# A linear-attention and expert-routing kernel: own terms moved to the scores' diagonal, router logits from turned outputs, state product on quarters of the array

## The chip, the cores and the metric

The kernel runs on one core of a Trainium2 chip. The time is the device time of one execution in microseconds (us); three runs of the kernel before gave a median of 439.97 us (439.43 to 441.21). The engines named below are PE (TensorE, the matrix engine; PEld is its loading of weights), DVE (VectorE), ACT (ScalarE), POOL (GpSimd) and SP (SyncE, which here only issues transfers). All data is fp32.

## The reference, cut to what matters

```python
# attention part: B=4, H=8 heads, S=768 tokens, D=48
for t in range(S):
    kt, vt, rt = k[:, :, t], v[:, :, t], r[:, :, t]
    cur = np.einsum('bhd,bhe->bhde', u[None] * kt, vt)          # the token's own term
    y[:, :, t] = np.einsum('bhd,bhde->bhe', rt, state + cur)
    state = w[None, :, :, None] * state + np.einsum('bhd,bhe->bhde', kt, vt)
x = y.transpose(0, 2, 1, 3).reshape(3072, 384)                  # a token's row: 8 heads of 48

# expert part: 4 groups of 4 experts, each 384 -> 1024 -> 384
g_idx = argmax(x @ w_group)                 # 384 x 4
e_idx = argmax(x @ w_expert[g_idx])         # 384 x 4 for each group
gate  = softmax of the group, at g_idx, times softmax of the expert, at e_idx
out   = gate * (relu(x @ w1[g_idx, e_idx]) @ w2[g_idx, e_idx])
```

The attention is computed in chunks of 128 tokens. Within a chunk, token t takes from an earlier token j of the chunk a score (r_t against k_j with decays) times v_j; from earlier chunks it takes r_t against the state; from itself it takes (sum over d of r*u*k) times v_t. That last part is the own term.

## The kernel before

There are 24 tiles (6 chunks of 4 batches), each of 128 tokens and 8 heads. The program runs in steps; in step s it works on several tiles at once, each at another stage: `turn(s)`, `scores(s-1)`, `values(s-2)`, `back(s-3)`, `rows_T(s-4)` and `row_logits(s-5)`. Two heads of 64 padded rows share the 128 rows of a tile; HP = 4 is the number of such pairs, DP = 64 the padded width of a head, P = 128, KO = 3.

```python
def own(g):                                    # for a pair of tiles; on POOL
    nc.gpsimd.tensor_mul(dg, rts[...], kts[...])
    nc.gpsimd.tensor_mul(dg, dg, spread(ub, 1, 2))
def own_sum(g):
    nc.vector.reduce_sum(out=du, in_=dg, axis=AX)
def own_values(n):                             # the own term, one per head: 8 on ACT
    for h in range(H):
        nc.scalar.mul(dv[:, h, :], v[:, a, h, 0:D], du[:, a, h : h + 1])

def turn(n):                                   # 8 transposes
    transposes of r into pr, of k into pk
    nc.vector.tensor_mul(rT, pr, T1T[m])
    nc.scalar.copy(kT, pk)

def scores(n):
    for hc in range(HP):
        for e in range(2):
            nc.tensor.matmul(pa[e][:, hc, :], lhsT=kT[rows of e, hc, :], rhs=rT[rows of e, hc, :])
    for e in range(2):
        nc.vector.tensor_mul(am[:, e], pa[e], spread(later, 1, HP))   # keeps earlier tokens only

def values(n):
    if c > 0:                                  # the state's part: four products on the whole array
        for hc in range(HP):
            nc.tensor.matmul(py[:, hc, :], lhsT=R[b][:, hc, :], rhs=rT[:, hc, :], ...)
    for hc in range(HP):
        for e in range(2):
            nc.tensor.matmul(py[64 * e : 64 * (e + 1), hc, :], lhsT=v of head 2hc+e, rhs=am[:, e, hc, :])
    nc.scalar.copy(yT, py)
    ...                                        # not in the last chunk: the state's update
    8 products into pu (64 rows x 48 columns)
    for e in range(2):
        nc.vector.tensor_add(state of e, pu[rows of e], state of e)   # or add and multiply

def back(n):
    4 transposes of yT into pb
    nc.vector.tensor_add(xts[c][:, b, 0:DM], pb, dv)                  # here the own term comes in
def rows_T(n):
    3 transposes of the row tile into px
    nc.scalar.copy(xT, px)
def row_logits(n):                             # 384 x 20 weights of the router, in three parts
    for ko in range(KO):
        nc.tensor.matmul(pl, lhsT=xT[:, ko, :], rhs=gw[:, ko, :], ...)
```

Every four tiles (in the last chunk every two) the router runs: `choice` (some 12 DVE instructions), `exps` (ACT), `before` (two PE products that count tokens), `gate` and `place` (8 DVE instructions), and `rows` (one indirect transfer on POOL for each tile, which writes token rows into the regions of their experts). After the last tile come, with `up(0, ...)` and `down(0, ...)`, the first 128 rows of the fullest expert, which were already written, and then sixteen items of up to 256 rows, one for each expert. PSUM tiles of the tag `bank` share six buffers in turn.

Of the kernel before, what the change touches and what calls it, by code (L numbers as in the profile page):

```python
# [15 lines left out]
P = 128  # L16
# [18 lines left out]
def kernel(  # L35
# [105 lines left out]
    def load_pair(g, k_queue=nc.sync):  # L141

        load(r, g, rts[g % RING][:, :, :, 0:D])
        load(k, g, kts[g % RING], k_queue)
        load(v, g, vts[g % (RING + 1)][:, :, :, 0:D])
# [21 lines left out]

    idle = bank([P, P], "idle")
# [19 lines left out]
    R = ring([P, HP, P], "R", B)  # L188
# [92 lines left out]
    gw = cst([P, KO, NL], "gw")  # L281

    def load_small():
        nc.sync.dma_start(out=gw[:, :, 0:G], in_=moe_w_group.rearrange("(ko p) g -> p ko g", p=P))
        for g in range(G):
            nc.sync.dma_start(
                out=gw[:, :, G + Eg * g : G + Eg * (g + 1)], in_=moe_w_expert[g].rearrange("(ko p) e -> p ko e", p=P)
            )
# [60 lines left out]
    def route(pool, rb, xt, T, sums, number, group, apart=False):  # L349
# [28 lines left out]
        def choice():  # L378
            nc.vector.reduce_max(out=mx, in_=L, axis=AX)

# [4 lines left out]
            nc.vector.reduce_max(out=kx, in_=key, axis=AX)  # L385
            nc.vector.tensor_tensor(out=ohg, in0=key[:, :, 0, :], in1=spread(kx[:, :, 0], 2, Eg), op=OP.is_equal)
# [5 lines left out]
            nc.vector.tensor_sub(ex, L, spread(mx, 3, Eg))  # L392
# [41 lines left out]
        return choice, exps, before, gate, place, rows  # L434
# [10 lines left out]
    w2_parts = wpool.tile([P, FO, KO, P], FP32, name="w2_parts")  # L445

# [22 lines left out]
    def logits(xT, pl):  # L469
        for ko in range(KO):  # L470
            nc.tensor.matmul(pl, lhsT=xT[:, ko, :], rhs=gw[:, ko, :], start=(ko == 0), stop=(ko == KO - 1))
# [78 lines left out]
    def up(i, f, beside=None):  # L550
# [15 lines left out]

        behind = {2: (0,), 4: (2,), 6: (4, 6)} if i > 1 else {4: (0, 2), 6: (4, 6)}
        if i != 1:
            w2 = weights[ITEMS[i][0]][1]
            for a in behind.get(f, ()):  # L570
                nc.scalar.copy(w2_parts[:, a : a + 2], w2[:, a : a + 2, :].rearrange("p f (c k) -> p f k c", k=KO))  # L571
# [74 lines left out]
    dgs, dvs = {}, {}  # L646
    rkT, ams, yTs, xts, lgs, xTs = {}, {}, {}, {}, {}, {}
# [5 lines left out]
    def own(g):  # L653

        dg = dgs[g] = pool.tile([P, 2, H, D], FP32, tag="dg", name="dg")
        nc.gpsimd.tensor_mul(dg, rts[g % RING][:, :, :, 0:D], kts[g % RING])  # L656
        nc.gpsimd.tensor_mul(dg, dg, spread(ub, 1, 2))

    def own_sum(g):
        du = dvs[g] = pool.tile([P, 2, H], FP32, tag="du", bufs=2, name="du")  # L660
        nc.vector.reduce_sum(out=du, in_=dgs.pop(g), axis=AX)  # L661

    def own_values(n):
        g, a = n // 2, n % 2
        dv = dvs[g, a] = pool.tile([P, H, D], FP32, tag="dv", bufs=4, name="dv")
        for h in range(H):
            nc.scalar.mul(dv[:, h, :], vts[g % (RING + 1)][:, a, h, 0:D], dvs[g][:, a, h : h + 1])  # L667
# [17 lines left out]
    def scores(n):  # L685
        kT, rT = rkT[n]
        am = ams[n] = pool.tile([P, 2, HP, P], FP32, tag="am", bufs=2, name="am")
# [8 lines left out]
        for e in range(2):  # L696
            nc.vector.tensor_mul(am[:, e], pa[e], spread(later, 1, HP))  # L697

    def values(n):
# [5 lines left out]
        py = bank([P, HP, P], "py")  # L705
        if c > 0:
            for hc in range(HP):
                nc.tensor.matmul(
                    py[:, hc, :], lhsT=R[b][:, hc, :], rhs=rT[:, hc, :], start=(hc == 0), stop=False,
                    skip_group_check=True,  # L710
                )
        for hc in range(HP):
            for e in range(2):
                nc.tensor.matmul(  # L714
                    py[DP * e : DP * (e + 1), hc, :], lhsT=vt[:, a, 2 * hc + e, :], rhs=am[:, e, hc, :],
                    start=(c == 0), stop=True, skip_group_check=True,
                )
        yT = yTs[n] = pool.tile([P, HP, P], FP32, tag="yT", bufs=2, name="yT")
        nc.scalar.copy(yT, py)
# [9 lines left out]
        for e in range(2):  # L729
            rows = slice(DP * e, DP * (e + 1))  # L730
            state = R[b][rows, :, DP * e : DP * e + D]
            if c == 0:
                nc.vector.tensor_copy(state, pu[rows])
            elif c % SPAN < SPAN - 1:
                nc.vector.tensor_add(state, pu[rows], state)
            else:
                nc.vector.tensor_add(pu[rows], pu[rows], state)
                nc.vector.tensor_mul(state, pu[rows], spread(w_span[rows, :], 2, D))

    def back(n):  # L740

        c, b = tiles[n]
        yT = yTs.pop(n)
        if b == 0:
            xts[c] = pool.tile([P, B, XW], FP32, tag="xt", bufs=3, name="xt")
        pb = bank([P, HP, 2, DP], "pb")
        for hc in range(HP):
            nc.tensor.transpose(pb[:, hc].rearrange("p e d -> p (e d)"), yT[:, hc, :], ident)  # L748
        nc.vector.tensor_add(
            xts[c][:, b, 0:DM].rearrange("p (h d) -> p h d", h=H), pb.rearrange("p a e d -> p (a e) d")[:, :, 0:D],  # L750
            dvs.pop((n // 2, n % 2)),
        )

    def rows_T(n):
        xTs[n] = pool.tile([P, KO, P], FP32, tag="xT", bufs=2, name="xT")
        c, b = tiles[n]
        transposed(xts[c][:, b, 0:DM].rearrange("p (k d) -> p k d", d=P), xTs[n])
# [6 lines left out]
    def row_logits(n):  # L764
        last, i = GROUP[n]
        if i == 0:
            lgs[last] = route_bank()
        logits(xTs.pop(n), lgs[last][:, NL * i : NL * (i + 1)])
# [14 lines left out]
    own(0)  # L783
# [9 lines left out]
    LAST = 4  # L793
    for s in range(NT + LAST):
# [7 lines left out]
        if s % 2 == 0 and s // 2 + 2 < NP:  # L802
            load_pair(s // 2 + 2)
        if s == 1:
            load_small()
        if s in (3, 5, 7, 9):
            zero_places(s // 2 - 1)
        if s == FOUR * B + 6:
            pieces.append(("last", pick_first))
        if s == FOUR * B + 7:  # L810
# [3 lines left out]
        if s == FOUR * B + 10:  # L814
            columns(0)
        run("first")
        if s < NT:
            turn(s)
            if s % 2 == 1 and s // 2 + 1 < NP:
                if s > 1:  # L820
                    scale_k(s // 2 + 1, nc.gpsimd)
                own(s // 2 + 1)
        for n in range(NT):
            if s == n + 2 and n < NT - 1:
                own_values(n)
        run("choice")
        if 0 <= s - 4 < NT:
            rows_T(s - 4)
        n = s - 5
        if 0 <= n < NT:  # L830
            row_logits(n)
        if s == NT + LAST - 1:
            up(0, 2)
            row_logits(NT - 1)
        if 0 <= s - 3 < NT:
            back(s - 3)
# [3 lines left out]
        if s == FOUR * B + 7:  # L840
            load_rows(0, first, nc.sync)
            load_w2(first, 0)
            weights[0] = places[0]
        if 0 <= s - 1 < NT:
            scores(s - 1)
        if s == NT:
            own_values(NT - 1)
        if s == 1:
            own_sum(0)
        if s % 2 == 0 and 0 < s // 2 < NP:  # L850
            own_sum(s // 2)

# [9 lines left out]
        for n in (n, NT - 1) if s == NT + LAST - 1 else (n,):  # L862
            if n not in ROUTED:
                continue
            choice, exps, before, gate, place, rows = routing(n)
            T = ROUTED[n]
# [307 lines left out]
```

## Time and profile before

| what | value |
|---|---|
| time, median of 3 | 439.97 us |
| span of the profiled execution | 438.3 us |
| PE busy | 420.7 us (96%) |
| DVE busy | 187.6 us (43%) |
| ACT busy | 208.1 us (47%) |
| POOL busy | 198.8 us (45%) |
| first transposes of the last tile, first product of the first full item | 136.69 us, 172.31 us |

The page gives the busy time of each engine, the span cut into 40 slices with the busy share of each in tenths, and groups of instructions with their number, mean time and what they waited for. The timeline lists instructions by time: start, time to the end of the group, engine, line, operation, output and inputs, number. The ends of matrix products are modelled, and products overlap; so what counts in the timeline of PE is the distance between starts, not the length. A product of fp32 shows as two MATMUL records, a transpose as one. The attention takes roughly the first 150 us of the span, the experts the rest.

### The profile page before, as it was taken

What the parts mean: (1) busy time and instruction counts of PE and PEld (TensorE: products, weight loads), DVE (VectorE), ACT (ScalarE), POOL (GpSimd) and SP (SyncE); (2) the same over time, 40 slices, a digit from 0 to 9 for tenths busy, and PEclk for the clock granted to TensorE, in tenths of its full rate; (3) what the DMA queues carried; (4) which work ended last, traced back from release to release, by engine and by line L of the source; (5) the groups of instructions that cost most, each with busy time, mean ns of one, the idle gap of its engine ahead of it and who ended that gap; (6) DMA issues with size and microseconds to landing.
All of it is one profiled execution on the core that took longest, in us unless ns stands there. A gap on an engine that the chain in (4) does not pass through costs nothing. (4 is left out here: it accounts for less than half of the span.)

```text
span 438.3 us, 9515 instructions
## 1 busy us (share of the span) xinstructions
PE 420.7 (96%) x3463; PEld 406.4 (93%) x3463; DVE 187.6 (43%) x616; ACT 208.1 (47%) x482; POOL 198.8 (45%) x209
## 2 busy tenths in 40 slices
PE   6899999999999879999999999999999999999994
PEld 6788999999999879979999999999999999999993
DVE  6576578878777665312230330331331330332011
ACT  1885565555556524251542624615625633552560
POOL 7856546757474052421533614425425524532451
PEclk9999999999999999999999999999999999999998
DMA  9999999981014665999999998899998899999300
GB/s 169 233 251 218 275 270 204 216 162 38 20 38 118 163 247 118 270 212 234 269 221 233 260 257 203 228 239 215 240 254 207 237 266 214 250 264 220 123 24 27
DMA packets 126417, 86.63 MB, mean 198 GB/s; under 512 B 98982, under 2 KB 115509, under 8 KB 126364
## 3 DMA queue, kind: packets, MB, share of 16 engines
q1 hardware_dynamic: 114732, 69.08, 70.2%
q0 software_dynamic: 4960, 9.48, 7.1%
q10 hardware_dynamic: 6672, 7.41, 5.2%
q8 instruction: 28, 0.46, 0.5%
q14 instruction: 25, 0.20, 0.2%
HBM read 70.15 MB, written 16.44 MB: 198 GB/s over the span
## 5 line engine op out<-in xcount | busy, mean ns | idle before, releaser
L624 POOL DMA_INDIRECT out_dram<-yp,ids x104 | 101.1, 972 | 158.3 <-DVE yo L579 122.8
L585 PE MATMUL po<-hT,w_parts 128*128 128x128 f32 (+15 forms) x816 | 138.0, 328 | 1.6 <-ACT hT L565 1.0
L585 PEld LDWEIGHTS po<-hT,w_parts 128*128 128x128 f32 x816 | 133.5, 191 | 3.6 <-ACT hT L565 1.8
L617 DVE STREAM_TRANSPOSE yr<-yo 128x224 f32<-128x224 f32 (+3 forms) x48 | 21.9, 461 | 168.2 <-ACT yo L588 168.2
L561 PE MATMUL ph<-xe,w 128*128 128x128 f32 (+7 forms) x432 | 71.7, 326 | 0.8 <-PE pb L748 0.8
L561 PEld LDWEIGHTS ph<-xe,w 128*128 128x128 f32 x432 | 69.5, 194 | 1.3 <-PE pb L748 1.0
L588 ACT COPY yo<-po 128x128 f32<-128x128 f32 (+15 forms) x51 | 16.3, 320 | 112.2 <-PE po L585 112.2
L561 PE MATMUL ph<-xe,kall 128*128 128x240 f32 (+7 forms) x384 | 67.1, 335 | 0.0
L561 PEld LDWEIGHTS ph<-xe,kall 128*128 128x128 f32 x384 | 65.2, 190 | 0.6
L565 ACT ACTIVATE hT<-ph 128x256 f32<-128x256 f32 (+15 forms) x68 | 33.1, 494 | 39.1 <-PE ph L561 38.9
L667 ACT ACTIVATE dv<-vt,du 128x48 f32<-128x48 f32 x192 | 45.9, 324 | 1.8 <-DVE du L661 1.8
L571 ACT COPY w_parts<-rall 128x768 f32<-128x768 f32 x32 | 38.1, 1239 | 4.0 <-DMA rall<-in_moe_w_dram 4.0
L571 ACT COPY w_parts<-w 128x768 f32<-128x768 f32 x32 | 37.9, 1236 | 0.4 <-DMA w<-in_moe_w_dram 0.4
L427 POOL DMA_INDIRECT x_sorted<-xt,place_i x24 | 23.7, 988 | 24.8 <-DVE xe L526 12.9
L697 DVE TENSOR_TENSOR am<-pa,later 128x512 f32<-128x512 f32 x48 | 30.9, 685 | 8.9 <-PE pa L692 8.6
L656 POOL TENSOR_TENSOR dg<-rall,kall 128x768 f32<-128x768 f32 x12 | 21.8, 1821 | 25.2 <-DVE du L661 25.2
L651 POOL TENSOR_TENSOR kh<-kall,T 128x768 f32<-128x768 f32 (+1 forms) x12 | 21.5, 1798 | 18.7 <-DMA kall<-in_k_dram 14.2
L682 ACT COPY kT<-pk 128x512 f32<-128x512 f32 x24 | 14.0, 584 | 33.6 <-PE pk L678 27.8
L692 PE MATMUL pa<-rT,kT 48*128 48x128 f32 x384 | 28.4, 285 | 0.4 <-DVE rT L680 0.4
L714 PE MATMUL py<-am,vt 128*64 128x128 f32 x384 | 26.5, 279 | 0.0
L692 PEld LDWEIGHTS pa<-rT,kT 48*128 48x128 f32 x384 | 23.6, 187 | 2.2 <-DVE rT L680 0.6
L714 PEld LDWEIGHTS py<-am,vt 128*64 128x64 f32 x384 | 20.7, 136 | 3.2 <-issue 0.7
(139 smaller groups left out, 449.7 us busy)
## 6 DMA issues: line engine op xcount, KB each, us to landing
w<-in_moe_w_dram SPq DMA_DIRECT2D x32, 384.0 KB, 7.8
w<-in_moe_w_dram SPq DMA_DIRECT2D x8, 1536.0 KB, 7.0
kall<-in_moe_w_dram SPq DMA_DIRECT2D x32, 384.0 KB, 8.1
rall<-in_moe_w_dram SPq DMA_DIRECT2D x8, 1536.0 KB, 12.4
x_sorted<-nothing ACTq DMA_DIRECT2D x4, 1544.0 KB, 7.3
rall<-in_r_dram SPq DMA_DIRECT2D x12, 384.0 KB, 8.2
vt<-in_v_dram SPq DMA_DIRECT2D x12, 384.0 KB, 6.5
kall<-in_k_dram SPq DMA_DIRECT2D x10, 384.0 KB, 6.7
```

Of the source, the lines that this page charges most:

```text
L427: ins = nc.gpsimd.indirect_dma_start(out=xs_dram, out_offset=bass.IndirectOffsetOnAxis(ap=place_i[:, i : i + 1], axis=0), in_=xt[:, i, :], ...
L561: nc.tensor.matmul(ph[:, q, :], lhsT=w1[:, ko, P * (f + q) : P * (f + q + 1)], rhs=xe[:, ko, 0:w], start=(ko == 0), stop=(ko == KO - 1), s ...
L565: nc.scalar.activation(hTs[i][:, f : f + 2, 0:w], ph, AF.Relu)
L571: nc.scalar.copy(w2_parts[:, a : a + 2], w2[:, a : a + 2, :].rearrange("p f (c k) -> p f k c", k=KO))
L585: nc.tensor.matmul(po, lhsT=w2_parts[:, fo, d, :], rhs=hT[:, fo, 0:w], start=(fo == 0), stop=(fo == FO - 1))
L617: nc.vector.transpose(yr[:, 0:b, :, d], y[:, d, 0:w].rearrange("p (b t) -> p b t", t=BL))
L624: ins = nc.gpsimd.indirect_dma_start(out=out_pieces, out_offset=bass.IndirectOffsetOnAxis(ap=ids[:, j : j + 1], axis=0), in_=yp[:, j], in_ ...
L656: nc.gpsimd.tensor_mul(dg, rts[g % RING][:, :, :, 0:D], kts[g % RING])
L667: nc.scalar.mul(dv[:, h, :], vts[g % (RING + 1)][:, a, h, 0:D], dvs[g][:, a, h : h + 1])
L692: nc.tensor.matmul(pa[e][:, hc, :], lhsT=kT[rows, hc, :], rhs=rT[rows, hc, :], start=True, stop=True, skip_group_check=True,)
L697: nc.vector.tensor_mul(am[:, e], pa[e], spread(later, 1, HP))
L714: nc.tensor.matmul(py[DP * e : DP * (e + 1), hc, :], lhsT=vt[:, a, 2 * hc + e, :], rhs=am[:, e, hc, :], start=(c == 0), stop=True, skip_gr ...
```

## The change

Four things are done together.

- The own term goes onto the diagonal of the scores: ACT writes `ident * du` (8 instructions of 128 columns) into the score tile beforehand, and the DVE then copies the scores over it only where the token is earlier (`copy_predicated` in place of the multiplication with the mask). The output of `values` is then complete, and nothing has to be added in `back`.
- As yT is complete, the router's logits are taken from it: four products with weights of 32 columns, each on its own group of 32 columns of the array, one copy, one transpose and one DVE sum. The three transposes of the rows, their copy and three products go away, and with them one step of the pipeline (LAST = 3).
- The state is kept as 64 x 64 blocks, and its product runs as eight products on the four quarters of the array; yT is copied in two halves, the state's update is one instruction for 128 rows and not two for 64.
- `choice` is split into `choice` and `expert`, in two steps; the exponentials come after them. The end of the program is ordered anew; the router's weights are loaded earlier and in ten transfers of 48 partitions.

```diff
-def own_values(n):
-        for h in range(H):
-            nc.scalar.mul(dv[:, h, :], vts[...][:, a, h, 0:D], dvs[g][:, a, h : h + 1])
+def own_scores(n):
+        am = ams[n] = pool.tile([P, 2, HP, P], FP32, tag="am", bufs=2, name="am")
+        for e in range(2):
+            for hc in range(HP):
+                h = 2 * hc + e
+                nc.scalar.mul(am[:, e, hc, :], ident, dus[n // 2][:, n % 2, h : h + 1])
 # scores
-            nc.vector.tensor_mul(am[:, e], pa[e], spread(later, 1, HP))
+            nc.vector.copy_predicated(am[:, e], earlier, pa[e])
 # values
-            for hc in range(HP):
-                nc.tensor.matmul(py[:, hc, :], lhsT=R[b][:, hc, :], rhs=rT[:, hc, :], ...)
+            for j in range(2):
+                for o in range(2):
+                    for e in range(2):
+                        rows = slice(DP * e, DP * (e + 1))
+                        nc.tensor.matmul(py[e][DP * o : DP * (o + 1), j, :],
+                            lhsT=R[b][rows, 2 * o + j, :], rhs=rT[rows, 2 * o + j, :], ...)
 ...
-        nc.scalar.copy(yT, py)
+        for e in range(2):
+            nc.scalar.copy(yT[:, :, e, :], py[e])
 ...
-        for e in range(2):
-            ... nc.vector.tensor_add(state, pu[rows], state)
+        state = R[b][:, :, 0:D]
+        ... nc.vector.tensor_add(state, pu, state)
 # back
+        pl = bank([P, P], "pl")
+        for j in range(HP):
+            nc.tensor.matmul(pl[BL * j : BL * (j + 1), :], lhsT=gw[:, j, :], rhs=yT[:, j, :], start=True, stop=True)
+        nc.scalar.copy(lgT, pl)
 ...
-        nc.vector.tensor_add(xts[c][:, b, 0:DM], pb, dvs.pop(...))
+        nc.vector.tensor_copy(xts[c][:, b, 0:DM], pb)
-def rows_T(n): ...
 # row_logits
-        logits(xTs.pop(n), lgs[last][:, NL * i : NL * (i + 1)])
+        by_block = lgs[last][:, 512 - P : 512]
+        nc.tensor.transpose(by_block, lgTs.pop(n), ident)
+        nc.vector.reduce_sum(out=lgs[last][:, NL * i : NL * (i + 1)], in_=by_block by columns, axis=AX)
 # the loop over steps
-    LAST = 4
+    LAST = 3
+            if s == 0:
+                own(0, nc.vector, 0, 1)
+                own_sum(0, 0, 1)
+                own(0, nc.gpsimd, 1, 2)
-            load_pair(s // 2 + 2)
+            load_pair(s // 2 + 2, between=load_small if s == 0 else None)
 ...
+        if s == NT + 1:
+            for a in (0, 2):
+                w2_part(0, a, nc.gpsimd.tensor_copy)
```

Left out here: the places of the router's parts in the steps, the rest of the order at the end, and the changes of a branch that runs only when the decays are out of range.

## The prediction

> **What bounds the kernel now.** I read the slices of the span first, then the busy times of the attention stage, then one step of PE in the timeline, then the end of the attention.
>
> ```profile
> PE   6899999999999879999999999999999999999994
> DVE  6576578878777665312230330331331330332011
> ACT  1885565555556524251542624615625633552560
> ...
> 20.00:120.00 100.00, 98.93 (x1293) 93.09 (x1293) 74.71 (x185) 59.39 (x202) 58.66 (x38) 1.00 0.86 189
> ```
>
> A slice is 11 us. PE is full from slice 3 on, with a dent in slices 14 and 15 (153 to 175 us), where the attention hands over to the experts. From 20 to 120 us PE is busy 98.9 of 100 us, DVE 74.7, ACT 59.4, POOL 58.7. So the attention is bound by PE, with DVE next. From 172 us on nothing is changed. Now one step of PE:
>
> ```profile
> 70.40 0.66 PE L678 MATMUL pr<-ident,rall 128*128 128x128 f32 x4
> 70.89 0.60 PE L678 MATMUL pk<-ident,kh 128*128 128x128 f32 x4
> 71.33 0.49 PE L466 MATMUL px<-ident,xt 128*128 128x128 f32 x3
> 71.66 0.74 PE L471 MATMUL rb<-gw,xT 128*128 128x20 f32 x6
> 72.25 0.63 PE L748 MATMUL pb<-ident,yT 128*128 128x128 f32 x4
> 72.72 1.06 PE L708 MATMUL py<-rT,R 128*128 128x128 f32 x8
> 73.70 1.09 PE L714 MATMUL py<-am,vt 128*64 128x128 f32 x16
> 74.63 0.62 PE L725 MATMUL pu<-vt,kh 128*64 128x48 f32 x16
> 75.18 1.16 PE L692 MATMUL pa<-rT,kT 48*128 48x128 f32 x16
> 76.27 0.44 PE L678 MATMUL pr<-ident,rall 128*128 128x128 f32 x2
> ```
>
> A step takes 76.27 - 70.40 = 5.87 us. The distances between starts give the rate: 0.44 us for four transposes is 0.11 a pass; the products with R need about 0.11 a pass; the router's rb, only 20 columns wide, also need 0.59 / 6 = 0.10. py and pa run two passes at a time (16 in about 8 x 0.11), pu, 48 wide, in about 8 x 0.058. The rest is change of shape. Here are the last passes of pu and the first of pa:
>
> ```profile
> 75.02 0.23 PE L725 MATMUL pu<-vt,kh 128*64 128x48 f32 x2
> 75.18 0.38 PE L692 MATMUL pa<-rT,kT 48*128 48x128 f32 x2
> ```
>
> The first pa passes are 0.38 us long where a later one has 0.27, so in effect they begin at 75.29, 0.27 after the last pu. The same reading gives 0.26 from R to py and 0.27 from pa to pr. Passes of one shape follow at 0.11, so each change of the array's shape costs about 0.15 us.
>
> The sum for a step, in passes of 0.11: turn 8 (0.88), px and rb with their transitions 0.95, pb 4 (0.44), R 8 (0.90), py 8 pairs (0.88), pu 0.47, pa 8 pairs (0.90), and three changes of shape (0.45): 5.87. It closes.
>
> **What the Trainium skill says.** "TensorEngine Tiling (Array Packing)", section Key Properties: "Changing tiling mode (not just tile) drains the TensorE", while different tiles of one mode run in parallel. The trace agrees: 0.26 us against 0.11. "TensorE: Matmul & The Clock Gate", section LDWEIGHTS: loading goes by the columns of the weights, not by rows; a load of 128 columns would be 107 ns by it (an estimate of that page). The trace agrees with 0.10 for the 20-wide rb. "ScalarE: Activation LUTs", section What ACT_TABLE_LOAD costs: 186 ns + 0.833 a column, 93 more for a scale read per partition, 93 overlapped; 128 columns then take 386 ns. The trace has 0.396 for such instructions (rev) and 0.324 for the 48-wide dv. "VectorE: DVE Perf Modes", the perf-mode tier table: with an operand in PSUM tensor_tensor runs at one element a cycle; the trace has 0.685 for am. For copy_predicated no page gives a rate; I take the same 0.685.
>
> **The change part by part, on PE in a step.** px and rb go: -0.95. R in quarters: sixteen passes, four at a time, 4 x 0.11 = 0.44, so -0.46. The logits pl: eight passes on four column groups, 2 x 0.11 = 0.22. The turned logits: one transpose, 0.11. But the shape now changes seven times, not three: turn to pl, pl to pb, pb to R, R to py, pu to the logits' transpose, that to pa, pa to turn. Four more at 0.15: +0.60. Net -0.95 - 0.46 + 0.22 + 0.11 + 0.60 = -0.48, a step of 5.39. So over half of what the packing saves goes to drains. In the first chunk (steps 2 to 5) there is no R: -0.95 + 0.33 + 3 x 0.15 = -0.17.
>
> ACT in a step: kT 0.58, eight own scores of 0.296 spacing and 0.4 for the last (2.5, before 1.9), two halves of yT at about 0.35 (before 0.58), lgT 0.27 (before xT 0.46). About 4.0 of 5.39 us, still off the path. DVE: two predicated copies, rT, a copy in place of the addition (0.5), one state update in place of two (-0.35), a sum over 80 elements (+0.24): 4.3 of 5.39 us. Its order fits: the predicated copies end about 1.4 us into the next step, and PE wants their banks for py at 1.97 us and their values at 2.6.
>
> From step 6 to 23: 18 steps x -0.48 = -8.6 us. Router steps: the three groups of four steps from 46.21 to 118.70 us took 0.4 to 0.9 us more than 4 x 5.87. With shorter steps the eight DVE instructions of gate and place (1.7 us) hold the predicated copies longer than PE can hide; I add 0.25 us for each of four groups: +1.
>
> **The start.** The first tile's own sums now stand before its scores: on DVE two products and a sum after rT (10.05 us), to about 12.2; then ACT, behind kT and rev, writes the eight own scores from 13.1 to 15.6; then the predicated copies. py of the first tile began at 14.87 and moves to about 16.3, and pl in step 3 waits for a yT that ACT writes behind a second set of own scores (about 21). ACT was already 80% busy from 20 to 30 us. The router's weights are needed in step 3, not in step 5; their transfers are put ahead of v, and k before them lands at about 20, so they come just in time. I take step 6 to begin 1.5 us later than its 33.89: +1.5.
>
> **The end.** From step 24 (142.11) to the first full item:
>
> ```profile
> 142.11 0.55 PE L466 MATMUL px<-ident,xt 128*128 128x128 f32 x3
> ...
> 161.42 0.38 PE L399 MATMUL pre<-ohe,later 128*128 128x32 f32 x2 [1.94 <-DVE rb L389]
> 161.89 3.58 PE L561 MATMUL ph<-xe,w 128*128 128x128 f32 x18
> ...
> 165.77 0.97 POOL L427 DMA_INDIRECT x_sorted<-xt,place_i  x1 [0.30 <-issue]
> ...
> 171.84 0.70 DVE L526 STREAM_TRANSPOSE xe<-xg 128x128 f32<-128x128 f32 x3 [3.54 <-DMA xg<-x_sorted]
> 172.31 5.53 PE L561 MATMUL ph<-xe,w 128*128 128x128 f32 x48
> ```
>
> That is 30.2 us, and it ends with the last tile's rows: logits, choice, count, place, two indirect writes, 2 us until the rows are loaded (168.7), 3 us of loading, the DVE transposes. After the change there are three steps, not four: PE work of about 4.5, 4.8 and 2.5 us up to the last logits (11.8); then DVE with choice and expert 2.7, count 0.7, gate and place 1.7, two writes 2.3 with their start, then 2.0 + 3.1 + 0.5 as in the trace: 24.8. One us is added for DVE transposes of the first 128 rows, which now stand early in step 24, where their rows may not be there. So 26 against 30.2: -4.
>
> **Sum.** +1.5 - 8.6 + 1 - 4 = -10.1, so 439.97 - 10 = 430 us.
>
> **The rivals.**
> - The drains eat it all. If a quarter or a column group does not run four at a time but two at a time, as py and pa do, R stays at 0.9 and pl takes 0.44: a step gains nothing (-0.48 + 0.46 + 0.22 = +0.20). Then 439.97 + 1.5 + 3.6 + 1 - 4 = 442. For it: nothing in this profile has four at once. Against it: pu shows that loads of weights to two column groups run side by side (0.058 a pair), as do row groups in pa.
> - DVE becomes the bound. It has some 1.1 us of room in a step. If a predicated copy takes twice 0.685, it needs 5.7 us, and with its waits the step is no shorter than before: about 437 to 439.
> - The start costs more. If the router's weights come behind the zero writes to the sorted rows, which share the DMA engines, step 3 stalls until 24 us: 2 to 3 us more, 432 to 433.
> - The end gives less: weights copied by POOL or the early transposes hold the chain: 432.
> - It gives more: the drain of a short block (lgT, pl) may be partly hidden, 0.1 a step, and the end has 5 us to give: 426.
>
> **Range and chances.** The steps and the end pull the same way, and only the first two rivals cancel them; I give those two 20% together. The limit of 2% is 431.2, just above my number, so a slightly dearer start moves it to "within". Predicted 430, range 424.5 to 437.5; faster by over 2% 0.56, within 0.38, slower by over 2% 0.06.
>
> **What would show it.** Starts of pr in the middle some 5.4 us apart; four starts of R passes close together and about 0.11 to the next four; 0.26 from the last pass of a shape to the first of the next, seven times; predicted copies of about 0.69; step 6 at about 35.4; from the last step with transposes to the first full item some 4 us less. I am wrong if the step stays near 5.9 (no packing by four, or DVE waits ahead of py), if the predicated copies run above 1 us, or if PE stands for long in step 3.

## The result: 435.3 us, a gain of 4.7 where 10 were expected

| | before | after |
|---|---|---|
| time, median | 439.98 us (4 runs, 439.43 to 441.21) | 435.30 us (4 runs, 434.65 to 436.64) |
| ratio to before, 95% interval | 1 | 0.9894 (0.9862 to 0.9925) |
| first turn of PE (step 0) | 8.95 | 8.58 |
| step 3 begins | 17.43 | 20.30 |
| step 6 begins | 33.89 | 44.22 |
| a plain step | 5.87 | 5.39 |
| step 23 begins | 136.69 | 137.39 |
| first full item (products ph of 5 us) | 172.31 | 167.73 |
| span of the profile | 438.3 | 432.9 |

The rows of steps and of the full item are starts of `pr`, or of `ph`, in the PE timelines of the two profiles; a plain step is the distance between two of them. Taken apart at these marks, the change of the span is: start up to step 6 +10.33; steps 6 to 23 -9.63 (102.80 to 93.17); step 23 to the first full item -5.28 (35.62 to 30.34); the experts behind it -0.82. The sum is -5.40. So what stands behind step 6 gave 15.7 us, more than the 11.6 that were expected, and the start took 10.3 of it back.

The slices of the span of the changed kernel, 10.8 us each, and the row of busy times from 20 to 120 us (columns: stretch, its length, busy us of PE, PE's loads, DVE, ACT, POOL with the number of instructions, granted clock, share of the DMA engines, GB/s):

```profile
PE   6749999999999989999999999999999999999993
DVE  6726678878797956123032130330330331232011
ACT  1847676767666541154261642633633643552460
...
PEclk9869999999999989999999999999999999999997
```

```profile
20.00:120.00 100.00, 94.38 (x1405) 77.25 (x1403) 70.20 (x184) 66.29 (x222) 58.40 (x39) 0.96 0.90 194
```

The third digit of PE, 21.6 to 32.5 us, is a 4 where the kernel before has a 9, and PEclk has a 6 in the same place: PE stands, and then works at a lower clock. From slice 4 on PE is full again, now with less work in each step; DVE has not become the bound (70.2 of 100 us, before 74.7). The dent at the hand-over to the experts is one slice in place of two.

One step of PE after the change:

```profile
55.00 0.66 PE L703 MATMUL pr<-ident,rall 128*128 128x128 f32 x4
55.49 0.60 PE L703 MATMUL pk<-ident,kh 128*128 128x128 f32 x4
56.02 0.43 PE L776 MATMUL pl<-yT,gw 128*32 128x128 f32 x8
56.37 0.66 PE L786 MATMUL pb<-ident,yT 128*128 128x128 f32 x4
56.96 0.67 PE L738 MATMUL py<-rT,R 64*64 64x128 f32 x16
57.56 1.09 PE L745 MATMUL py<-am,vt 128*64 128x128 f32 x16
58.48 0.62 PE L757 MATMUL pu<-vt,kh 128*64 128x48 f32 x16
59.03 0.33 PE L805 MATMUL rb<-ident,lgT 128*128 128x128 f32 x1
59.29 1.16 PE L717 MATMUL pa<-rT,kT 48*128 48x128 f32 x16
60.38 0.43 PE L417 MATMUL rb<-ohe,later 128*128 128x64 f32 x2
```

From 55.00 to 60.38 is 5.38 us, and the plain step before it 5.39 (the last line is the router's count, which stands ahead of the next turn here). pl with its eight passes takes 0.35 from start to start, R with sixteen 0.60 where eight took 0.98. Each of these blocks contains a change of shape, as was counted.

And step 3, in which the start is lost:

```profile
20.30 1.11 PE L703 MATMUL pr<-ident,rall 128*128 128x128 f32 x4
21.21 0.95 PE L703 MATMUL pk<-ident,kh 128*128 128x128 f32 x4
27.77 0.66 PE L776 MATMUL pl<-yT,gw 128*32 128x128 f32 x8 [5.62 <-DMA gw<-in_moe_w_expert_dram]
28.36 1.12 PE L786 MATMUL pb<-ident,yT 128*128 128x128 f32 x4
29.41 1.98 PE L745 MATMUL py<-am,vt 128*64 128x128 f32 x16
31.17 1.04 PE L757 MATMUL pu<-vt,kh 128*64 128x48 f32 x16
...
33.76 0.66 PE L703 MATMUL pr<-ident,rall 128*128 128x128 f32 x4
```

PE stands 5.62 us for the router's weights, gw. Then pb takes 1.12 us where it takes 0.66 in the step at 55 us, py 1.98 for 1.09, pu 1.04 for 0.62: the same products at about half the clock. This is what the Trainium skill, "TensorE: Matmul & The Clock Gate", Part 1, describes (half clock after an idle window, full clock again after a busy one); the granted clock was 0.53 from 25 to 30 us and 0.78 from 30 to 35. The page gives the idle window as about 3.4 us; in this trace shorter stands did it too: after py of tile 0 had waited 1.47 and 0.46 us (16.2 to 17.3 us), the clock was 0.50 from 20 to 21 us.

SP's transfers in this stretch, and the first write of zeros to the sorted rows, 1544 KB, which ACT issues (columns: start and length of the issue):

```profile
13.18 1.48 SPq L136 DMA_DIRECT2D kall<-in_k_dram  x1
14.79 1.90 SPq L178 DMA_DIRECT2D gw<-in_moe_w_group_dram  x1
16.73 1.90 SPq L180 DMA_DIRECT2D gw<-in_moe_w_expert_dram  x4
18.68 1.43 SPq L178 DMA_DIRECT2D gw<-in_moe_w_group_dram  x1
20.15 1.95 SPq L180 DMA_DIRECT2D gw<-in_moe_w_expert_dram  x4
20.84 0.40 ACTq L354 DMA_DIRECT2D x_sorted<-nothing  x1
22.15 1.27 SPq L136 DMA_DIRECT2D vt<-in_v_dram  x1
```

Ten transfers of 192 pieces of 16 bytes; the last is issued at 22.1, when pl already wants it, and v of the third pair only after that. While the later ones are issued the DMA engines do little: 26 GB/s from 18 to 20 us and 3 GB/s from 20 to 21. Then the zeros and v fill them, with 411 GB/s from 22 to 24 us, and the last of the ten, issued by 22.1, lets pl begin only at 27.8.

The end, from the last count to the first full item:

```profile
157.13 0.41 PE L417 MATMUL pre<-ohe,later 128*128 128x32 f32 x2 [1.39 <-DVE ohe L407]
...
161.53 0.98 POOL L445 DMA_INDIRECT x_sorted<-xt,place_i  x1 [0.30 <-issue]
...
167.36 0.70 DVE L548 STREAM_TRANSPOSE xe<-xg 128x128 f32<-128x128 f32 x3 [3.34 <-DMA xg<-x_sorted]
...
167.73 1.49 PE L583 MATMUL ph<-xe,w 128*128 128x128 f32 x11 [0.58 <-DVE xe L548]
```

It is the same chain as before (count, last row write, rows loaded, transposed), 4.2 to 4.6 us earlier. In the kernel before, PE was busy with other products until the rows were there; now it waits 0.58 us for them.

### The profile page after: what moved, and what is told of

Same layout as the page of the kernel before. It is cut to its first block, busy times and chain, and to the rows that moved or that the text cites. A ratio compares the mean times of both kernels' runs of the same rounds, so it can differ in the third digit from the quotient of the medians.

```text
span 432.9 us, 9886 instructions
## 1 busy us (share of the span) xinstructions
PE 411.8 (95%) x3623; PEld 383.1 (88%) x3623; DVE 185.6 (43%) x620; ACT 214.3 (50%) x504; POOL 199.8 (46%) x211
## 5 line engine op out<-in xcount | busy, mean ns | idle before, releaser
L607 ACT COPY yo<-po 128x128 f32<-128x128 f32 (+15 forms) x51 | 16.3, 321 | 113.7 <-PE po L604 113.7
L692 ACT ACTIVATE am<-ident,du 128x128 f32<-128x128 f32 x192 | 58.8, 393 | 3.8 <-DVE du L684 3.6
L722 DVE COPY_PREDICATED am<-later,pa 128x512 f32<-128x512 uint32 x48 | 32.5, 728 | 13.8 <-PE pa L717 10.5
L678 POOL TENSOR_TENSOR dg<-rall,kall 128x768 f32<-128x768 f32 (+1 forms) x12 | 21.4, 1786 | 36.5 <-DVE du L684 30.8
L467 ACT COPY w_parts<-w 128x768 f32<-128x768 f32 x30 | 35.7, 1239 | 0.0
L745 PE MATMUL py<-am,vt 128*64 128x128 f32 x384 | 27.4, 285 | 1.9 <-DVE am L722 1.9
L717 PEld LDWEIGHTS pa<-rT,kT 48*128 48x128 f32 x384 | 24.6, 192 | 2.9 <-ACT kT L707 0.2
```

Source lines behind the costliest of these rows:

```text
L692: nc.scalar.mul(am[:, e, hc, :], ident, dus[n // 2][:, n % 2, h : h + 1])
L717: nc.tensor.matmul(pa[e][:, hc, :], lhsT=kT[rows, hc, :], rhs=rT[rows, hc, :], start=True, stop=True, skip_group_check=True,)
L722: nc.vector.copy_predicated(am[:, e], earlier, pa[e])
L745: nc.tensor.matmul(py[e][DP * o : DP * (o + 1), j, :], lhsT=vt[:, a, 4 * o + 2 * j + e, :], rhs=am[:, e, 2 * o + j, :], start=(c == 0), st ...
```

## The experiments

In two of the four groups of runs the kernel before itself took 460.6 and 464.3 us, so a kernel is compared by its ratio to the kernel before of its own group, and by the marks of its trace up to step 22.

| kernel | time, us | ratio to before (95%) | first turn to step 6 | first turn to step 7 | steps 6 to 22 |
|---|---|---|---|---|---|
| before | 439.98 | 1 | 24.95 | 31.39 | 97.05 |
| after | 435.30 | 0.9894 (0.9862 to 0.9925) | 35.64 | 41.03 | 88.24 |
| after_again | 461.14 | 0.9929 (0.9894 to 0.9963) | 35.85 | 41.24 | 88.66 |
| own_before | 468.34 | 1.0193 (1.0115 to 1.0271) | 26.23 | 32.10 | 100.64 |
| zero_later | 432.62 | 0.9824 (0.9791 to 0.9857) | 33.92 | 39.31 | 88.86 |
| gw_act | 436.39 | 0.9914 (0.9888 to 0.994) | 34.30 | 39.69 | 88.23 |
| warm3 | 435.05 | 0.9868 (0.9817 to 0.9919) | 33.85 | 39.24 | 88.23 |
| pl_later | 451.95 | 0.9784 (0.9682 to 0.9885) | 27.28 | 38.30 | 94.27 |
| pl_later_reorder | 453.16 | 0.9895 (0.9791 to 0.9999) | 25.66 | 39.10 | 93.93 |
| spread | 430.29 | 0.9764 (0.9732 to 0.9795) | 29.92 | 35.31 | 88.24 |
| spread_zero | 431.17 | 0.9775 (0.9736 to 0.9814) | 27.43 | 33.08 | 91.87 |
| r_same | 459.79 | 0.9978 (0.9936 to 1.002) | 35.62 | 41.03 | 88.88 |
| joined | 444.25 | 1.0093 (1.0065 to 1.0121) | 36.38 | 41.77 | 91.29 |
| reorder | 431.91 | 0.9819 (0.9755 to 0.9883) | 34.20 | 39.29 | 84.44 |
| spread_zero_reorder | 427.46 | 0.9703 (0.9687 to 0.9719) | 25.39 | 32.57 | 87.86 |
| spread_reorder | 450.19 | 0.9732 (0.9598 to 0.9866) | 25.39 | 32.58 | 88.65 |

The first turn itself began anywhere from 8.6 to 10.5 us, with the landing of the first r; that is why the start is counted from it. Kernels with gw's products deferred do some of the work of steps 3 and 4 in steps 5 and 6, so step 7 is the fair mark for them.

**Is the loss at the start the kernel's own?** The changed kernel once more, unedited.

> The changed kernel itself once more, nothing edited. If the wait for the router's weights belongs to the kernel: pl of step 3 at 27 to 29.5 us again with 4 to 6 us of wait on gw, step 6 at 43.5 to 45.5 us, ratio to before 0.986 to 0.993. If it was an accident of the one profiled execution: pl at 23 us or earlier, step 6 before 40 us.

The first turn to step 6 took 35.85 us, and pl of step 3 began at 29.14, 18.0 us after the turn of step 1 against 17.2 in the first profile; PE stood 7.35 us there:

```profile
29.14 0.66 PE L776 MATMUL pl<-yT,gw 128*32 128x128 f32 x8 [7.35 <-DMA x_sorted<-nothing]
```

The wait is put down to the zero write, which landed last. The loss belongs to the kernel.

**Which part of it is the own scores' chain?** One part of the change alone, in the kernel before:

```diff
-            nc.vector.tensor_mul(am[:, e], pa[e], spread(later, 1, HP))
+            nc.vector.copy_predicated(am[:, e], earlier, pa[e])
...
+    def own_scores(n):   # as in the changed kernel; own_values and dv go
...
-        nc.vector.tensor_add(xts[c][:, b, 0:DM]..., pb..., dvs.pop((n // 2, n % 2)))
+        nc.vector.tensor_copy(xts[c][:, b, 0:DM]..., pb...)
```

> The kernel before with one part of the change alone: own scores on the diagonal by ACT, predicated copies in place of the product with the mask, a plain copy in back; transposes of x, rb, R over 128 rows, choice and the router's weights stay as before. Theory A (this part costs the start its 2.9 us by the own-score chain and nothing in a step): py of tile 0 at 16 to 17 us (14.87 before), step 6 at 36 to 37, plain steps 5.87 as before, time 442 to 443. Rival (the part is free at the start, and the 2.9 us also come from the router's weights pushing v and r back): step 6 at 34 to 34.5, time 440 to 440.5. If the predicated copies at 0.73 us made DVE the bound, steps would be over 6.0 us and the time above 443.

The start became 1.3 us longer up to step 6 and 0.7 up to step 7, and plain steps stayed at 5.87. So up to step 6 the chain costs at most about what the prediction's 1.5 had for it: in this execution PE also ran at half clock in its first two turns (pk 1.06 us for 0.60). Step 3 itself began 2.8 us later after the first turn than before the change (11.31 against 8.48), but it took 4.67 us in place of 6.52. What was not expected is the ratio: steps 6 to 22 took 100.64 us in place of 97.05. ACT's waits from 30 to 150 us in this kernel (columns: total us, times, longest), and its instructions in one of the steps concerned, say why:

```profile
ACT ex L395 <- DVE ex L392: 17.0, 4, 4.9
```

```profile
59.47 0.27 ACT L395 ACTIVATE ex<-ex 128x80 f32<-128x80 f32 x1 [4.03 <-DVE ex L392]
59.65 0.18 ACT L396 COPY xt<-tok 128x4 f32<-128x4 f32 x1
59.73 0.47 ACT L467 COPY xT<-px 128x384 f32<-128x384 f32 x1
60.10 2.44 ACT L673 ACTIVATE am<-ident,du 128x128 f32<-128x128 f32 x8
62.45 0.56 ACT L725 COPY yT<-py 128x512 f32<-128x512 f32 x1
```

ACT stands 4.03 us at the exponentials for DVE's choice; the own scores come only behind it, and with them the predicated copies and py; PE's next transposes of the outputs waited 1.08 us for yT, and the step was 7.1 us. In the kernel before ACT waited there too, 8.3 us in four waits, but PE stood for none of them; dv behind it is wanted only a step later, in `back`. Whether the change's other part, choice in halves and exponentials later, is what avoids this is the next experiment.

**The split undone.** In the changed kernel, for the groups of four tiles:

```diff
-            when = [(1, "choice"), (2, "choice"), (2, "last"), (3, "first"), (3, "last"), (3, "last")]
+            when = [(1, "choice"), (1, "choice"), (1, "choice"), (2, "first"), (2, "last"), (2, "last")]
```

> The changed kernel with the router's choice, its second half and the exponentials in one step again, as before the change, for the groups whose place in the steps was changed. In own_before, which has the own scores on ACT and the old router, ACT stood 4.0 us on the exponentials' operand, the own scores behind it came late, and each of the four such steps became 1.2 us longer. Theory A (the split is what keeps ACT free for the own scores): four steps longer by 1 to 1.3 us, PE waiting for yT or am behind ACT, time 4 to 5 us more than the changed kernel, ratio to before 0.998 to 1.001. Rival (the split only spreads DVE's work; the banks and lgT give enough slack): 0 to 1.5 us more, ratio 0.989 to 0.993.

It was 8.9 us more than the changed kernel. Steps 6 to 22 took 3.05 us more, 0.76 for each of the four groups: less than the 1 to 1.3 expected, since PE waits only for the count now (1.5 us in all), and more than the rival had. The step from 22 to 23 took 8.3 us in place of 4.9: the last group's row writes came a step earlier and stood on POOL ahead of the last kh, for which PE waited 1.68 us and lost its clock. The rest is a later first turn (1.9) and the start (0.7). So the split is worth about 3 us by itself, and a further 3 by the place of the row writes.

**The router's weights: three attempts that left the wait or moved it.** First the zero writes, the rival that the prediction named:

```diff
-        if s in (3, 5, 7, 9):
-            zero_places(s // 2 - 1)
+        if s in (5, 6, 8, 9):
+            zero_places({5: 0, 6: 1, 8: 2, 9: 3}[s])
```

> The changed kernel, but the four zero writes of 1.5 MB to the sorted rows are issued in steps 5, 6, 8 and 9 and not in 3, 5, 7 and 9; nothing else. Theory A (the start: in step 3 PE waits 5.6 us for the router's weights, whose last transfers, issued at 18.7 to 22.1 us, queue behind the first zero write, issued at 20.8; then the clock is low for a while): without the zero write the weights are there at about 23.5 us, the wait of pl falls from 5.6 to 1 to 2 us, and the whole is 4 to 6 us faster than the changed kernel's 435.3, 429.5 to 431.5. Theory B (the start is bound by something else as well, ACT's own scores or the loads of k, and only the name of the wait changes): under 2 us faster, 433.5 to 435.5.

PE still waited 4.34 us for gw, until 25.07. The wait is only 1.3 us shorter, but the zero write had a large part in the landing: the last of the ten was now issued at 23.2, and pl began 1.9 us behind it, where it was 5.7 with the zero write beside it. Counted from the first turn pl began 3.8 us earlier. Up to step 6 only 1.7 of that was left: PE worked at the lower clock for longer afterwards (pl to the next turn 6.79 us for 5.99, the step behind it 6.66 for 5.43). Two of the five-us windows of this kernel show the other part (second to last number: share of the DMA engines; last: GB/s):

```profile
15.00:20.00 5.00, 3.71 (x57) 3.06 (x56) 2.91 (x6) 5.00 (x17) 2.45 (x3) 1.00 1.16 159
20.00:25.00 5.00, 0.74 (x7) 0.50 (x5) 2.84 (x4) 2.06 (x7) 5.00 (x3) 0.94 0.23 23
```

While PE waits for gw, the DMA engines are nearly idle: 23 GB/s. What takes the time here is the issuing of ten short transfers, one behind the other (15.6 to 23.2 us on SP, at least 0.44 us for each), with nothing large moving meanwhile. Then the same ten on ACT's queue at the very start:

```diff
-                nc.sync.dma_start(out=gw[rows, ...], in_=...)   # ten of them, between k and v of pair 2
+                nc.scalar.dma_start(out=gw[rows, ...], in_=...) # at the start, behind first_use
```

> The changed kernel, but the ten transfers of the router's weights are issued on ACT's queue at the very start, where ACT waits anyway (5 to 8.8 us), and not on SP's queue behind the second pair of tiles. Theory A: no wait for the weights at all, pl begins at about 22 us, right behind the turned output, PE never stands for 3 us, so the clock stays; step 6 begins at 36 to 37 us and not at 44.2, and the whole takes 427 to 429. Theory B: step 6 still begins after 41 us, held by ACT or by the load of k; 432.5 to 435.

A miss: pl no longer waited for gw, but the issues held ACT from 3.30 to 17.0 us:

```profile
15.05 1.96 ACTq L180 DMA_DIRECT2D gw<-in_moe_w_expert_dram  x4
17.05 0.48 ACT L285 COPY T<-ptab 128x384 f32<-128x384 f32 x1 [12.34 <-DMA vt<-in_v_dram]
```

kh waited for T, pk of step 0 began at 18.18, and step 6 came at 44.35. The wait is put down to the landing of v, and the first of the ten issues alone took 4.74 us; that they stood behind larger transfers is likely, but no run shows it. The Trainium skill, "DMA: Bandwidth & Descriptors", Issuing engines are not separate DMA queues, says that another issuing engine only saves the sequencer's time to initiate a DMA, "usually small relative to the DMA itself"; here the ten issues, 30 KB in all, made T's copy wait 12.3 us. Third, the low clock alone: 52 passes of ones in front of pl in step 3, which keep PE busy and compute nothing of use.

```diff
+        if s == 3:
+            busy = bank([P, P], "busy")
+            for _ in range(26):
+                nc.tensor.matmul(busy, lhsT=ones, rhs=ones, start=True, stop=True)
```

> The changed kernel with 26 products of ones in front of pl in step 3, into a bank of their own: they fill the wait of 5.6 us and do nothing else. If the clock lowered after the wait costs time (py of step 3 has its 16 passes in 1.76 us and not in 0.93), PE is back at full speed at once and the whole is 2 to 2.5 us faster, 432.8 to 433.3. If the slow passes of step 3 come from waits for operands and not from the clock, there is no gain, 435.3, or a loss of 0.3 for the products that stand after the weights have come.

```profile
23.12 6.07 PE L876 MATMUL busy<-ones 128*128 128x128 f32 x52
29.12 0.42 PE L776 MATMUL pl<-yT,gw 128*32 128x128 f32 x8
29.48 0.66 PE L786 MATMUL pb<-ident,yT 128*128 128x128 f32 x4
30.06 1.09 PE L745 MATMUL py<-am,vt 128*64 128x128 f32 x16
```

pl to the next turn took 3.77 us (29.12 to 32.89) in place of 5.99 (27.77 to 33.76): the low clock costs 2.2 us of the start. Up to step 6, counted from the first turn, 1.8 us were gained (33.85 for 35.64), although the passes put pl 0.4 us later. In the time no gain shows: the two ratios lie within each other's intervals.

**The need moved instead of the transfer.** The products of the outputs of tiles 0 and 1 with gw are made in step 5, with those of tile 2:

```diff
+        if n < 2:
+            delayed.append(to_logits)     # pl and lgT, as they were
+        else:
+            while delayed:
+                delayed.pop(0)()
+            to_logits()
```

> The logits of tiles 0 and 1 are made in step 5 together with those of tile 2, so that the router's weights are needed at about 34 us and not in step 3; nothing else is changed. Theory A (the wait for the router's weights and the low clock that it leaves cost the start 8 of its 10 us): no wait of PE on gw, step 3 takes 3.5 to 4 us at full clock, step 6 begins at 36 to 38 us (44.2 in the changed kernel, 33.9 before), time 427 to 429. Theory B (the start is bound by the chain of the own scores on DVE and ACT and by v landing late behind the router's weights, and the wait on gw only shows the same delay): the wait turns into one for am, yT or v, step 6 begins after 41 us, time 433 or more.

Half of each theory was right. The wait for gw and the low clock were gone and step 6 began at 37.07. But then it stood itself:

```profile
38.46 1.80 POOL L671 TENSOR_TENSOR kh<-kall,T 128x768 f32<-128x768 f32 x1 [10.69 <-DMA kall<-in_k_dram]
...
40.32 1.11 PE L703 MATMUL pk<-ident,kh 128*128 128x128 f32 x4 [2.59 <-POOL kh L671]
```

POOL waited 10.69 us for k of pair 3, PE 2.59 for POOL, again at half clock afterwards, and step 7 began at 48.08, only 2.7 us better than in the changed kernel (38.30 against 41.03 from the first turn). In the kernel before, pair 3's kh began at 32.40. There are two suspects: the row of short transfers, which puts every later one back, and the second zero write, issued at 29.84, right behind this k (28.06).

> The later logits of tiles 0 and 1 together with the order that has five changes of shape in a step in place of seven. If the two gains are independent: steps of 5.09 us (-0.3 each), 3.4 us less than pl_later as the reordering gave by itself, so 424 to 425.5. If the reordering's gain and the start's are one (a later start hides part of it): 427 to 428.

With shorter steps as well (the edit is shown under reorder), step 6 came earlier (25.66) and step 7 did not (39.10): the same k bounds both. The time was inconclusive; its interval overlaps that of pl_later.

**The short transfers spread.** As pl_later, with the ten no longer in a row:

```diff
         load(r, g, rts[g % RING][:, :, :, 0:D])
+        small(3)          # up to three of the ten
         load(k, g, kts[g % RING], k_queue)
-        if between is not None:
-            between()     # all ten
+        small(3)
         load(v, g, vts[g % (RING + 1)][:, :, :, 0:D])
+        small(2)
```

> As pl_later, but the ten short transfers of the router's weights are no longer issued in a row: three stand behind r of pair 2, three behind its k, two behind its v, two behind r of pair 3. In pl_later the wait for the weights was gone (step 6 at 37.1 us), but step 6 itself then stood for k of pair 3, which landed at 38.4. Theory A (while ten transfers of 192 pieces of 16 bytes are issued in a row, nothing large is behind them and the DMA engines run dry, 0.46 of their time used from 20 to 25 us; all later transfers are late by that): DMA share at 20 to 25 us above 0.8, kh of pair 3 begins at 33 to 35.5 us, no wait in step 6, step 7 at 42 to 44 us (48.1 in pl_later), time 3 to 4 us less than pl_later's ratio gives. Theory B (k of pair 3 is late because of the second zero write, not because of the order of the short ones): kh of pair 3 stays at 37 us or later, step 7 at 46 or later, no gain over pl_later.

```profile
20.00:25.00 5.00, 5.00 (x32) 4.44 (x34) 3.29 (x6) 3.86 (x14) 4.92 (x4) 0.50 0.94 284
```

The DMA engines were at 0.94, 284 GB/s, pair 3's kh began at 33.06 and no longer waited for k, and step 7 came 35.31 us after the first turn, 3.0 less than in pl_later and 5.7 less than in the changed kernel. Its clock of 0.50 in this stretch has another cause: py of tile 0 waited 1.78 us for its scores. The slow steps also moved the second zero write to 32.86, out of the way of k, so this run alone does not part the two suspects. The pair pl_later_reorder and spread_reorder (below) parts them: with k of pair 3 issued at 27.8 and the second zero write at 29.6 and 29.9, kh began at 38.41 with the ten in a row, after a wait for k, and at 32.82 with the ten spread, without one:

```profile
32.82 1.82 POOL L683 TENSOR_TENSOR kh<-kall,T 128x768 f32<-128x768 f32 x1 [4.90 <-PE pl L791]
```

Theory A holds. The ratio fell to 0.9764.

> As spread, and the four writes of zeros to the sorted rows are issued in steps 5, 6, 8 and 9 in place of 3, 5, 7 and 9. Theory A: little more than spread, step 7 at 42 to 43 us, within 1 us of it. Theory B: here and only here kh of pair 3 begins before 34 us and step 7 at 42 to 43.

Step 7 at 33.08, better by 2.2. It is not shown that this is the zero writes' doing: the 1.78 us wait and the half clock of spread from 20 to 26 us are missing here, and with the shorter steps below both places of the zero writes come to step 7 after 32.57 and 32.58 us. And ACT stood 6.89 us around the fourth of them, now in step 9:

```profile
59.63 0.38 ACTq L366 DMA_DIRECT2D x_sorted<-nothing  x1
60.11 0.58 ACT L719 COPY kT<-pk 128x512 f32<-128x512 f32 x1 [6.89 <-DMA rall<-in_r_dram]
```

PE waited 2.81 us for lgT behind it, and steps 6 to 22 took 3.6 us more than in spread; the time is that of spread.

**Packing by four.** The two products of one quarter issued one behind the other, in place of four different quarters in turn:

```diff
-            for j in range(2):
-                for o in range(2):
-                    for e in range(2):
+            for o in range(2):
+                for e in range(2):
+                    for j in range(2):
```

> The changed kernel with the sixteen quarter products of R issued so that the two of one quarter follow each other, in place of four different quarters in a row; the same products and results. Theory A (the gain of R comes from four quarters running at once): pairs on one quarter stand behind each other, R takes about 0.8 us in place of 0.44, a step 5.7 to 5.8 in place of 5.39, time 441 to 443. Rival (the order does not matter, PE takes each quarter's queue by itself): 5.39 and 435.

The rival was right: R took 0.62 from its start to that of py (0.60 in the changed kernel) and the step 5.41. Four quarters work side by side whichever order the products come in, so the order carries none of the gain.

**Fewer changes of shape.** pl behind pb, and the transpose of the logits behind the turns of the next step:

```diff
-        n = s - 3                 # row_logits ahead of scores
-        if 0 <= n < NT:
-            row_logits(n)
+        if 0 <= s - 4 < NT - 1:   # row_logits behind turn
+            row_logits(s - 4)
```

> The changed kernel with two moves on PE: pl behind pb, next to the state's quarters, and the transpose of the logits not between pu and pa but in the next step, right behind the eight transposes of turn; the last tile keeps its order. The same products, five changes of the array's shape in a step and not seven. If each change costs 0.15 us, as the prediction has it, a step falls from 5.39 to 5.09 us and the whole by 24 x 0.3 = 7 us, to 428. If the drains of short blocks are hidden or DVE is at its limit (1.36 us of predicated copies, 4.4 us of work in a step), the step stays at 5.3 or above and the whole is within 2 us of 435.3.

Plain steps took 5.09 us, 0.30 less for two changes, 0.15 each as it was counted. Steps 6 to 22 took 3.8 us less, not 16 x 0.30 = 4.8, since some became 5.2 to 5.4.

**Together.** spread_zero with the edit of reorder, and the same with the zero writes where the change has them:

> As spread_zero, with five changes of shape in a step in place of seven (products of the turned outputs with the router's weights behind the transposes of the outputs, transpose of the logits behind the turns of the next step). If the start stays as in spread_zero and steps are 5.1 us: step 7 at 41.5 to 42.5, the last step with transposes about 5 us earlier than in spread_zero, ratio to before 0.955 to 0.965. If DVE or ACT, or transfers of k, bound the shorter steps: steps of 5.3 and a ratio of 0.965 to 0.975.

This is the fastest: 427.46 us (426.82 to 428.33, 4 runs), 0.9703 of the kernel before, against 0.9894 for the changed one. Step 7 came 32.57 us after the first turn, 1.2 more than before the change and 8.5 less than after it. By its trace the second case of the expectation is the nearer one: steps 6 to 22 took 87.86 us, 7.2 of them in step 6, where PE waits 1.1 and 0.34 us for the three deferred logits' one bank.

> As spread_zero_reorder, but the writes of zeros stay in steps 3, 5, 7 and 9, where the changed kernel has them. In spread_zero ACT stood 6.9 us at the fourth write of zeros in step 9 and PE 2.8 us for lgT behind it; in spread nothing of the kind happened. If that stall is the price of the later writes: 425.5 to 427, ratio to before 0.965 to 0.970, step 10 reached by 57.5 us (59.0 in spread_zero_reorder). If the later writes help the start by as much as they cost there: the same as spread_zero_reorder, 427 to 428.5, ratio 0.970 to 0.973.

Step 10 began at 58.6, not by 57.5 (59.05 with the later zero writes), and the ratio's interval (0.9598 to 0.9866) contains that of the kernel with the later zero writes. Which place of the zero writes is better is left open.

## Why the prediction was wrong

| term | predicted | measured |
|---|---|---|
| start, up to step 6 | +1.5 | +10.3 |
| shorter steps, 17 from step 6 to 23 | -8.2 (17 x 0.48) | -8.2 (5.87 to 5.39) |
| router steps | +1 | -1.5 |
| step 23 to the first full item | -4.5 (its -4, and one step more) | -5.3 |
| behind it | 0 | -0.8 |

**The step that failed** is the start: "The router's weights are needed in step 3, not in step 5; their transfers are put ahead of v, and k before them lands at about 20, so they come just in time." They came at 27.8. The rival beside it ("step 3 stalls until 24 us: 2 to 3 us more") had half of the mechanism and too small a size: the weights did land behind a zero write, but without it PE still waited 4.34 us. What the runs showed in place of "just in time": ten short transfers in a row take SP over 7 us to issue, the DMA engines run nearly dry meanwhile, and the zero write then takes the engines while the last of them is still to land; PE waits 5.6 us, and the half clock behind it costs 2.2 more. With the need deferred, step 6 came 8.4 us sooner after the first turn (27.28 for 35.64), but then k of pair 3 was late, because of the row again. Spreading the ten as well brought back 5.7 of the 9.6 us up to step 7, and 8.0 with the zero writes moved too (whether the last 2.2 are theirs is open). The rest, 1.7, holds the own scores' chain, at most 0.7 to 1.3, which the prediction's +1.5 was for, and the deferred products; py of tile 0 began at 16.22 (16.3 was predicted).

The trace of the kernel before had it. Its five transfers of the weights, issued at 17.88, were not all issued before 24.85, and no wait showed, because step 5 began at 28.94:

```profile
17.88 2.66 SPq L284 DMA_DIRECT2D gw<-in_moe_w_group_dram  x1
20.58 4.27 SPq L286 DMA_DIRECT2D gw<-in_moe_w_expert_dram  x4
```

With the need moved to 22 us and the number doubled, "just in time" could not hold.

**The steps** were right, term by term: the step is 5.39, R in quarters takes four passes at a time, a change of shape costs 0.15, and the rival of packing by two is out by the R block (0.60 with its change of shape, where eight passes and a change took 0.98). DVE as the bound is out too: the predicated copies took 0.728 us each, pairs 1.33, against 0.685 taken for one.

**The router steps** were mis-sized and of the wrong sign. Beyond plain steps the stretch from 6 to 23 took 3.0 us before (102.80 - 17 x 5.87) and 1.5 after (93.17 - 17 x 5.39). The wait that the +1 stood for did not come: the four router steps are 0.49 us longer than a plain one (5.88 for 5.39, the last 6.10), as before (6.36 for 5.87, one 6.80), which is about the count's own products (0.50 from the first of them to the next turn), and the profile shows no wait of PE from step 6 to step 23. The prediction did not see ACT's wait at the exponentials either, which would have made these steps longer; the split avoids it (3.05 us over four groups when undone). The -1.5 lies mainly in single steps (step 6 took 6.45 before and 5.39 after, step 22 5.75 and 4.93) and was not taken apart.

**The end** gave 0.8 more than its term. No run takes it apart.

## What to carry to other kernels

When a consumer moves earlier, read from the trace when its transfer was last issued and not only when it was last missed: a wait that does not show may have been covered by a few us. A row of short transfers costs issue time on an in-order queue, and everything large behind it is late by that; here it helped to put them in twos and threes between large ones, and it did not help to put them on an engine that computes. Where an engine's queue gets a new critical instruction (here the own scores on ACT), look for what stands ahead of it and waits.

## What was not expected of the hardware

- Ten transfers of 192 pieces of 16 bytes, 30 KB in all, held SP from 15.6 to 23.2 us (zero_later), with the DMA engines at 23 GB/s from 20 to 25; issued on ACT they held it until 17.0 us, and T's copy waited 12.3.
- After 5.6 us of standing, PE ran at about half clock (pb 1.12 for 0.66 us), which cost 2.2 us; in pl_later 2.6 us of standing brought it on as well (pk 1.11 for 0.60), and in the changed kernel two waits of 1.47 and 0.46 us (pa 1.99 for 1.16).
- Sixteen products on quarters took the same 0.60 to 0.62 us with the quarters in turn and with each quarter's four passes in a row.
